# Sliding-window attention and a feed-forward on one core: early loads in float32 on one queue, cast on chip; attention two tiles ahead

## The chip, the core and the metric

The kernel runs on one core of one Trainium2 chip. The metric is device microseconds of one execution. The profile's span (first to last instruction) is about 2 us shorter than that time; 373.34 us of time was a span of 371.6. The engines are named as the profile names them: PE is TensorE, PEld its weight loads, DVE is VectorE, ACT is ScalarE, POOL is GpSimd, SP is the engine that issues most DMAs. PSUM is where both kernels put the results of their matmuls and transposes (pt, ps_s, ps_od, ph and py in the timelines).

## The reference, cut to what matters

```python
# q, k, v: (8 batches, 8 heads, 576 positions, 64), float32
scores = (q @ k.T) / 8                       # per head
scores = where(|i - j| <= 32, scores, -1e9)  # sliding window
attn   = softmax(scores) @ v
x      = attn as (8*576 tokens, 512)
h      = x @ w_in                            # 512 x 2048
out    = gelu_tanh(h) @ w_out                # 2048 x 512, float32 out
```

## The kernel before

Attention works on a batch of 576 tokens, the feed-forward on tiles of 512 tokens. Batch 0's attention runs first, alone. Then tile t of the feed-forward runs with batch t+1's attention scattered between its matmuls. The traces show the work of an engine in the order in which the kernel issues it, so where an instruction is issued decides what it can hold up; x4 below moves the casts of a pair in that order and nothing else, and the pair's loop goes from 7.70 to 6.13 us.

One unit of attention is half of a pair of heads; a batch has four pairs, eight units. The parts that the change and the argument touch:

```python
def cast_pair(b, pr):                 # q and k of a pair, float32 -> float16
    ...
    nc.vector.tensor_copy(q16 or k16, raw q or k)           # two casts, 128x512

def trans_pair(b, pr):                # 8 transposes into one PSUM tile, 2 copies out
    pt = psT.tile([128, 8, 128], FP16, name="pt", tag="T")  # psT: one buffer
    for j in range(4): nc.tensor.transpose(pt[:, j, :], q16[:, j, :, :], idn)
    for j in range(4): nc.tensor.transpose(pt[:, 4 + j, :], k16[:, j, :, :], idn)
    nc.vector.tensor_copy(QTs[b][:, pr, :, 0:128], pt[:, 0:4, :])
    nc.vector.tensor_copy(KTs[b % 2]..., pt[:, 4:8, :]...)

def scores(b, u):                     # psS: one buffer
    ... 6 matmuls into ps_s
    nc.scalar.activation(pe, ps_s, AF.Exp, scale=SCALE)
    nc.vector.tensor_tensor(pm, pe, mask, op=ALU.mult)

def values(b, u):                     # psO: one buffer; row sums come from a matmul with ones
    ... 12 matmuls into ps_od
    nc.scalar.activation(lt, sums, AF.Ln)
    nc.scalar.activation(rt, lt, AF.Exp, scale=-1.0)        # 1 / sum
    nc.vector.tensor_tensor(xT[...], values, rt, op=ALU.mult)

# the start: batch 0
cast_tail(0)
for pr in range(NPAIR):
    cast_pair(0, pr)
    trans_pair(0, pr)
    if pr == 0:
        trans_tail(0)                 # positions 512..575 of all heads, same PSUM buffer
    for u in (2 * pr, 2 * pr + 1):
        scores(0, u)
        if u > 0:
            values(0, u - 1)
values(0, 7)

for t in range(NT):                   # 9 tiles
    b = t + 1
    # input half: 64 matmuls, with the casts and transposes of batch b between them
    # output half: 64 matmuls, with scores and values of batch b between them
    ...
```

q and k come on SP's queue in float32; v, w_in and w_out on GpSimd's queue, whose transfers write float16: a quarter of w_in is 512 KB in the page of before and 1024 KB in that of after, where it comes in float32, and both pages have 36.70 MB read from HBM.

The softmax here doesn't subtract the row's maximum and nothing guards it: scores larger than these inputs give would overflow.

## Time and profile before

| | |
|---|---|
| time | 373.57 us median of 3 runs (373.52 to 374.18) |
| profiled span | 371.6 us, PE busy 338.2 us (91%) |
| first feed-forward matmuls | three at 41.34 us; the rest from 42.88 us, after the last product xT |
| a tile with one batch of attention | 38.40 us, of which 37.88 busy |
| a tile without attention | 27.65 us |

The next lines are the busy time by stretch of the kernel before. The columns are the stretch in us, its length, then busy time and number of instructions of each engine, the granted TensorE clock, the DMA share and GB/s.

```profile
0.00:42.88 42.88, 17.68 (x184) 12.53 (x185) 19.11 (x46) 15.12 (x26) 19.41 (x37) 1.00 1.19 222
42.88:82.18 39.30, 39.23 (x313) 18.81 (x313) 18.17 (x41) 25.32 (x43) 6.90 (x9) 1.00 0.88 115
120.58:158.99 38.41, 37.89 (x310) 18.20 (x308) 18.96 (x42) 25.63 (x42) 4.81 (x7) 1.00 0.56 105
```

The number just after the comma, TensorE's busy time, is what to read: it is idle for 25 of the first 43 us, and for half a microsecond per tile afterwards. So only the start has time to take. What the start waits for is in the timeline of the kernel before. A line has start and duration in us, engine, source line, operation, output and inputs; the bracket is the engine's idle time before it and what ended it.

```profile
24.33 0.46 DVE L238 TENSOR_TENSOR xT<-ps_od,rt 128x288 f16<-128x288 f32 x1 [1.02 <-ACT rt L237]
24.70 0.42 DVE L174 CAST q<-qr 128x512 f16<-128x512 f32 x1
25.04 0.42 DVE L174 CAST k<-kr 128x512 f16<-128x512 f32 x1
25.18 0.61 PE L183 MATMUL pt<-idn,q 128*128 128x128 f16 x4 [1.80 <-DVE q L174]
...
26.25 0.42 DVE L186 COPY QT<-pt 128x512 f16<-128x512 f16 x1 [0.80 <-PE pt L185]
26.60 0.68 DVE L187 COPY KT<-pt 128x512 f16<-128x512 f16 x1
...
27.33 0.53 PE L201 MATMUL ps_s<-QT,KT 64*128 64x160 f16 x6 [1.12 <-DVE KT L187]
...
32.88 0.61 PE L183 MATMUL pt<-idn,q 128*128 128x128 f16 x4 [1.80 <-DVE q L174]
```

The q cast at 24.70 has no bracket: it starts as soon as VectorE is done with the product xT and waits for no data. TensorE in its turn waits 1.80 us for that cast. The pair's loop from transposes to transposes is 32.88 - 25.18 = 7.70 us, all of it latency of small instructions on three engines. The feed-forward follows the loop's end at once, as the chain of the kernel before shows (start, duration, what was worked on):

```profile
40.51 0.92 PE ps_od L228 x12
...
42.88 2.77 PE ph L254 x9
```

The nine matmuls from 42.88 us are not the first. The first twelve need xT, three of them only pairs that were done, and these three run while the last product is still being made. The timeline of the kernel before has all twelve, and then the transposes of batch 1's tail:

```profile
41.34 4.30 PE L254 MATMUL ph<-xT,w_in 128*128 128x512 f16 x12
45.49 0.39 PE L162 MATMUL pt<-idn,t 128*128 128x128 f16 x4
```

The prediction, and the expectations below, count the start of before as 42.88 us. Where this text compares starts, it takes the first matmul of each kernel, 41.34 us here.

### The profile page before, as it was taken

How to read it: one execution, taken by the hardware profiler on the slowest of the kernel's cores; microseconds unless marked ns; L12 is line 12 of the kernel's file. 1: busy time of each engine (PE TensorE's matmuls, PEld its weight loads, DVE VectorE, ACT ScalarE, POOL GpSimd, SP SyncE). 2: the span in 40 equal slices, each digit the busy share in tenths (PEclk: the TensorE clock that was granted, in tenths of full speed). 3: DMA queues.
4: the chain of work that ended last, by engine and by line, in shares of the span. 5: the costliest groups of instructions: out<-in, count | busy, mean ns of one | idle time of the engine just before them, and what ended most of it. 6: DMA issues, size and time to landing. Idle time of an engine off the chain costs nothing.

```text
span 371.6 us, 6392 instructions
## 1 busy us (share of the span) xinstructions
PE 338.2 (91%) x2592; PEld 164.6 (44%) x2592; DVE 156.8 (42%) x347; ACT 214.4 (58%) x352; POOL 45.6 (12%) x67
## 2 busy tenths in 40 slices
PE   0545799999999999999999999999999999999995
PEld 0334354445444444444444544454445444444442
DVE  2554453555354635553545445653545353011011
ACT  1234656676666766677666667656675677612600
POOL 8622121040002200120004000400000000000000
PEclk9999999999999999999999999999999999999999
DMA  9999999159223951197129801991020111013012
GB/s 156 268 246 205 247 211 76 59 67 255 56 56 47 226 105 59 31 201 145 30 58 170 179 28 59 146 202 30 28 58 0 30 30 57 2 30 84 2 37 76
DMA packets 72574, 37.64 MB, mean 101 GB/s; under 512 B 47456, under 2 KB 67936, under 8 KB 72544
## 3 DMA queue, kind: packets, MB, share of 16 engines
q1 hardware_dynamic: 30816, 28.32, 28.0%
q0 software_dynamic: 41728, 8.92, 26.4%
q8 instruction: 20, 0.33, 0.4%
q14 instruction: 10, 0.08, 0.1%
HBM read 36.70 MB, written 9.44 MB: 124 GB/s over the span
## 4 chain that ended last, share of the span: by engine, by line
PE 82%; ACT 9%; DVE 4%; POOL 3%; issue 1%; POOLq 0%
PE py L268 35%; PE ph L254 29%; PE ps_od L228 9%; PE ps_s L201 5%; ACT rt L237 3%; ACT lt L235 2%; ACT L258 2%; PE pt L185 2%; PE pt L183 2%; DVE xT L238 2%; ACT gT L258 1%; POOL V L107 1%; POOL w_in L120 1%; ACT pe L208 1%; POOL mask L129 1%
## 5 line engine op out<-in xcount | busy, mean ns | idle before, releaser
L268 PE MATMUL py<-w_out,gT 128*128 128x512 f16 x576 | 142.9, 381 | 0.0
L254 PE MATMUL ph<-xT,w_in 128*128 128x512 f16 x576 | 135.3, 382 | 3.6 <-ACT gT L258 3.1
L258 ACT ACTIVATE gT<-ph 128x512 f16<-128x512 f32 x144 | 84.5, 597 | 58.5 <-PE ph L254 57.5
L254 PEld LDWEIGHTS <-w_in 128*128 128x128 f16 x576 | 54.6, 98 | 65.2 <-issue 8.2
L208 ACT ACTIVATE pe<-ps_s 128x832 f16<-128x832 f32 x64 | 55.2, 862 | 37.5 <-PE ps_s L201 37.4
L268 PEld LDWEIGHTS <-gT 128*128 128x128 f16 x576 | 47.7, 98 | 51.9
L210 DVE TENSOR_TENSOR pm<-pe,mask 128x832 f16<-128x832 f16 x64 | 37.9, 592 | 61.1 <-ACT pe L208 60.5
L107 POOL DMA_DIRECT2D V<-in_v_dram x32 | 28.5, 894 | 184.2 <-PE ps_od L228 157.9
L235 ACT ACTIVATE lt<-ps_od 128x288 f32<-128x288 f32 x64 | 26.2, 410 | 40.7 <-PE ps_od L228 40.7
L238 DVE TENSOR_TENSOR xT<-ps_od,rt 128x288 f16<-128x288 f32 x64 | 29.3, 458 | 47.7 <-ACT rt L237 47.7
L272 DVE COPY yo<-py 128x512 f32<-128x512 f32 x36 | 24.7, 685 | 49.5 <-PE py L268 49.5
L228 PE MATMUL ps_od<-pm,V 128*64 128x192 f16 (+4 forms) x384 | 35.7, 242 | 4.6 <-DVE xT L238 3.9
L228 PEld LDWEIGHTS <-V 128*64 128x64 f16 x384 | 23.4, 115 | 29.5 <-issue 29.1
L228 PE MATMUL ps_od<-pm,ones 128*64 128x192 f16 (+4 forms) x384 | 32.9, 236 | 0.0
L186 DVE COPY QT<-pt 128x512 f16<-128x512 f16 x32 | 13.6, 425 | 43.1 <-PE pt L185 43.1
L237 ACT ACTIVATE rt<-lt 128x288 f32<-128x288 f32 x64 | 28.3, 443 | 2.0
L201 PE MATMUL ps_s<-QT,KT 64*128 64x192 f16 (+4 forms) x384 | 24.1, 235 | 4.7 <-DVE KT L187 3.3
L183 PE MATMUL pt<-idn,q 128*128 128x128 f16 x128 | 13.3, 230 | 15.2 <-DVE q L174 15.2
L201 PEld LDWEIGHTS <-KT 64*128 64x128 f16 x384 | 12.3, 97 | 29.8 <-issue 25.0
L228 PEld LDWEIGHTS <-ones 128*64 128x64 f16 x384 | 24.0, 117 | 0.0
L187 DVE COPY KT<-pt 128x512 f16<-128x512 f16 x32 | 21.8, 681 | 0.0
L183 PEld LDWEIGHTS <-q 128*128 128x128 f16 x128 | 10.0, 102 | 22.2 <-DVE q L174 15.6
(27 smaller groups left out, 108.1 us busy)
## 6 DMA issues: line engine op xcount, KB each, us to landing
qr<-in_q_dram SPq DMA_DIRECT2D x7, 1024.0 KB, 9.7
kr<-in_k_dram SPq DMA_DIRECT2D x7, 1024.0 KB, 13.6
V<-in_v_dram POOLq DMA_DIRECT2D x32, 128.0 KB, 8.3
w_in<-in_moe_w_in_dram POOLq DMA_DIRECT2D x4, 512.0 KB, 22.8
w_out<-in_moe_w_out_dram POOLq DMA_DIRECT2D x4, 512.0 KB, 30.1
out_dram<-yo SPq DMA_DIRECT2D x8, 256.0 KB, 2.3
out_dram<-yo SPq DMA_DIRECT2D x8, 224.0 KB, 2.4
out_dram<-yo SPq DMA_DIRECT2D x8, 192.0 KB, 2.3
```

What stands on the lines that cost most here:

```text
L107: nc.gpsimd.dma_start(V[:, c, :, :], v[b, :, 128 * c:128 * c + 128, :].rearrange("h p d -> p h d"))
L183: nc.tensor.transpose(pt[:, j, :], q16[:, j, :, :], idn)
L201: nc.tensor.matmul(ps[:, h, off:off + 4 * n].rearrange("k (j p) -> k j p", j=4), KTs[b % 2][r0:r0 + 64, pr, 128 * c:128 * c + 128], QTs[b] ...
L208: nc.scalar.activation(pe, ps[:, :, 0:SW], AF.Exp, scale=SCALE)
L210: nc.vector.tensor_tensor(pm, pe, masks[hf].rearrange("p (o w) -> p o w", o=1).broadcast_to([128, 2, SW]), op=ALU.mult)
L228: nc.tensor.matmul(od[r0:r0 + 64, w, 0:4 * HALF].rearrange("d (j p) -> d j p", j=4)[:, :, a:e], V[:, c, 2 * pr + h, :] if w == 0 else ones ...
L235: nc.scalar.activation(lt, od[:, 1, 0:4 * HALF], AF.Ln)
L237: nc.scalar.activation(rt, lt, AF.Exp, scale=-1.0)
L238: nc.vector.tensor_tensor(xT[:, pr, b * S:(b + 1) * S].rearrange("d (j p) -> d j p", j=4)[:, :, HALF * hf:HALF * hf + HALF], od[:, 0, 0:4 ...
L254: nc.tensor.matmul(ph, w_in16[:, dc, fc * 128:fc * 128 + 128], xT[:, dc, t * 512:(t + 1) * 512], start=(dc == 0), stop=(dc == 3))
L258: nc.scalar.activation(gTs[t][:, fc, :], ph, AF.Gelu_apprx_tanh)
L268: nc.tensor.matmul(py, gTs[t][:, fc, t4 * 128:t4 * 128 + 128], w_out16[:, fc, :], start=(fc == 0), stop=(fc == NF - 1))
```

## The change

Its intent: the early loads (q, k, v of two batches, w_in, w_out) come in float32 on SP's queue in the order in which they are needed, and are cast on chip, mostly on GpSimd. The attention of two batches runs before the feed-forward. The first two tiles share their input half group by group, so that each megabyte of w_in that arrives feeds two tiles. Later, batch t+2 runs within tile t, wholly in its output half. The diff, cut to its core:

```diff
-FIRST, LAG, STEP = 15, 4, 7
+FIRST, STEP, LAG = 8, 6, 10
+TRANS = (0, 13, 25, 37)
+RING = 2048                                  # xT becomes a ring of 2048 tokens
...
-    load_qk(0, 4)
-    load_v(0)                                # and w_in, w_out, batch 1: GpSimd's casting queue
+    load_qk(0, True)                         # by pair on SP: q, k, (tails), v
...
+    load_qk(1, True)
...
+    for b in range(2):
+        cast_tail(b)
+        for pr in range(NPAIR):
+            cast_pair(b, pr, nc.gpsimd)
+            nc.gpsimd.tensor_copy(V..., vr...)          # two casts
+            trans_pair(b, pr)
+            if pr == 0:
+                trans_tail(b)
+            for u in (2 * pr, 2 * pr + 1):
+                scores(b, u)
+                values(the unit before)
+    wi = [load_w_in(0)]
+    cast_w(wi[0], w_in16[:, :, 0:512])       # half VectorE, half GpSimd
+    values(1, 7)
+    for g in range(4):                       # input halves of tiles 0 and 1
+        for t in range(2):
+            for fc in range(4 * g, 4 * g + 4):
+                ffn_in(t, fc)
+                ...                          # next group's load and cast
+    ...                                      # w_out loads and casts, loads of batch 2
     for t in range(NT):
+        if t >= 2:
+            for fc in range(NF): ffn_in(t, fc)
+        b = t + 2
+        cast_tail(b); cast_pair(b, 0)
+        for pr in range(NPAIR):
+            put(TRANS[pr], trans_pair, b, pr)
+            if pr == 0: put(TRANS[pr] + 2, trans_tail, b)
+            if pr < 3:  put(TRANS[pr] + 4, cast_pair, b, pr + 1)
+        for u in range(8):
+            put(FIRST + STEP * u, scores, b, u)
+            put(FIRST + STEP * u + LAG, values, b, u)
+        for i in range(64):                  # output half
+            ...                              # what was put at step i
+            ffn_out(t, i)
```

More of the change, by code (lines that the diff above doesn't have):

```diff
@@ L67 @@
     gp = ctx.enter_context(tc.tile_pool(name="gp", bufs=2))
+    stage = ctx.enter_context(tc.tile_pool(name="stage", bufs=3))
     yp = ctx.enter_context(tc.tile_pool(name="yp", bufs=3))
@@ L84, with load_qk @@
     w_out16 = big.tile([128, NF, DM], FP16, name="w_out16")
-    xT = big.tile([128, NPAIR, NTOK], FP16, name="xT")
+    xT = big.tile([128, NPAIR, RING], FP16, name="xT")
     raws = {}
-    def load_qk(b, split):
+    def load_qk(b, by_pair):
         qr = rawp.tile([128, H, 256], FP32, name="qr")
@@ L93, in load_qk, with main, tail @@
         raws[b] = (qr, kr, tr)
-        step = H // split
-        for h0 in range(0, H, step):
+        def main(h0, h1):
             for src, dst in ((q, qr), (k, kr)):
                 nc.sync.dma_start(
-                    dst[:, h0:h0 + step, :],
-                    src[b, h0:h0 + step, 0:512, :].rearrange("h (p j) d -> p h (j d)", j=4))
-            if h0 == 0:
-                nc.sync.dma_start(tr[0:64, :, :], q[b, :, 512:576, :].rearrange("h s d -> s h d"))
-                nc.sync.dma_start(tr[64:128, :, :], k[b, :, 512:576, :].rearrange("h s d -> s h d"))
+                    dst[:, h0:h1, :],
+                    src[b, h0:h1, 0:512, :].rearrange("h (p j) d -> p h (j d)", j=4))
+        def tail():
+            nc.sync.dma_start(tr[0:64, :, :], q[b, :, 512:576, :].rearrange("h s d -> s h d"))
+            nc.sync.dma_start(tr[64:128, :, :], k[b, :, 512:576, :].rearrange("h s d -> s h d"))
+        if by_pair:
+            vr = stage.tile([128, 5, H, 64], FP32, name="vr", tag="stage")
+            raws[b] = (qr, kr, tr, vr)
+            for h0 in range(0, H, 2):
+                main(h0, h0 + 2)
+                if h0 == 0:
+                    tail()
+                for h in (h0, h0 + 1):
+                    nc.sync.dma_start(vr[:, 0:4, h, :],
+                                      v[b, h, 0:512, :].rearrange("(c p) d -> p c d", p=128))
+                nc.sync.dma_start(vr[0:64, 4, h0:h0 + 2, :],
+                                  v[b, h0:h0 + 2, 512:576, :].rearrange("h p d -> p h d"))
+        else:
+            main(0, H)
+            tail()
     def load_v(b):
@@ L112, with load_w_in, load_w_out, cast_w @@
     w_out_v = moe_w_out.rearrange("(c p) f -> p c f", p=128)
-    load_qk(0, 4)
+    def load_w_in(i):
+        w = stage.tile([128, 4, 512], FP32, name="wst", tag="stage", padded_shape=[128, 5, 512])
+        nc.sync.dma_start(w, w_in_v[:, :, 512 * i:512 * i + 512])
+        return w
+    def load_w_out(i):
+        w = stage.tile([128, 4, 512], FP32, name="wst", tag="stage", padded_shape=[128, 5, 512])
+        nc.sync.dma_start(w, w_out_v[:, 4 * i:4 * i + 4, :])
+        return w
+    def cast_w(w, dst):
+        for c in range(4):
+            (nc.vector if c < 2 else nc.gpsimd).tensor_copy(dst[:, c, :], w[:, c, :])
+    load_qk(0, True)
     nc.gpsimd.memset(idn, 0.0)
@@ L117 @@
                             base=0, pattern=[[-1, 128]], channel_multiplier=1)
-    load_v(0)
-    for i in range(4):
-        nc.gpsimd.dma_start(w_in16[:, :, 512 * i:512 * i + 512], w_in_v[:, :, 512 * i:512 * i + 512])
     for h in range(2):
@@ L138 @@
         assert off == SW
-    for i in range(4):
-        nc.gpsimd.dma_start(w_out16[:, 4 * i:4 * i + 4, :], w_out_v[:, 4 * i:4 * i + 4, :])
     nc.vector.memset(ones, 1.0)
@@ L144 @@
         nc.vector.memset(Vs[i][64:128, 4, :, :], 0.0)
-    load_qk(1, 1)
-    load_v(1)
+    load_qk(1, True)
     halfs = {}
@@ L167, in trans_tail, with cast_pair @@
         nc.vector.tensor_copy(KTs[b % 2][:, :, 512:576], pt[:, :, 64:128])
-    def cast_pair(b, pr):
-        qr, kr, tr = raws[b]
+    def cast_pair(b, pr, eng=None):
+        qr, kr = raws[b][0:2]
         q16 = ap_.tile([128, 4, 2, 64], FP16, name="q16")
@@ L173, in cast_pair @@
         for src, dst in ((qr, q16), (kr, k16)):
-            nc.vector.tensor_copy(
+            (eng or nc.vector).tensor_copy(
                 dst.rearrange("p j h d -> p h j d"),
@@ L189, in trans_pair, with ring_pieces @@
             pt[:, 4:8, :].rearrange("d j p -> d p j"))
+    def ring_pieces(b, hf):
+        rows = []
+        for j in range(4):
+            g, a = b * S + j * NP_ + HALF * hf, 0
+            while a < HALF:
+                pos = (g + a) % RING
+                e = min(HALF, a + RING - pos)
+                rows.append([j, j + 1, a, e, pos])
+                a = e
+        out_rows = []
+        for r in rows:
+            o = out_rows[-1] if out_rows else None
+            if o and o[2:4] == r[2:4] and o[1] == r[0] and r[4] == o[4] + (o[1] - o[0]) * NP_ \
+                    and o[4] + (r[1] - o[0]) * NP_ <= RING:
+                o[1] = r[1]
+            else:
+                out_rows.append(r)
+        return out_rows
     units = {}
@@ L237, in values @@
         nc.scalar.activation(rt, lt, AF.Exp, scale=-1.0)
-        nc.vector.tensor_tensor(
-            xT[:, pr, b * S:(b + 1) * S].rearrange("d (j p) -> d j p", j=4)[:, :, HALF * hf:HALF * hf + HALF],
-            od[:, 0, 0:4 * HALF].rearrange("d (j p) -> d j p", j=4),
-            rt.rearrange("d (j p) -> d j p", j=4), op=ALU.mult)
+        o3 = od[:, 0, 0:4 * HALF].rearrange("d (j p) -> d j p", j=4)
+        r3 = rt.rearrange("d (j p) -> d j p", j=4)
+        for (j0, j1, a, e, pos) in ring_pieces(b, hf):
+            n, w = j1 - j0, e - a
+            if n > 1:
+                dst = xT[:, pr, pos:pos + n * NP_].rearrange("d (j p) -> d j p", p=NP_)[:, :, 0:w]
+            else:
+                dst = xT[:, pr, pos:pos + w].rearrange("d (j p) -> d j p", j=1)
+            nc.vector.tensor_tensor(dst, o3[:, j0:j1, a:e], r3[:, j0:j1, a:e], op=ALU.mult)
     gTs = {}
@@ L254, in ffn_in @@
             nc.tensor.matmul(ph, w_in16[:, dc, fc * 128:fc * 128 + 128],
-                             xT[:, dc, t * 512:(t + 1) * 512],
+                             xT[:, dc, t * 512 % RING:t * 512 % RING + 512],
                              start=(dc == 0), stop=(dc == 3))
@@ L282, in ffn_out @@
                 g = e
-    cast_tail(0)
-    for pr in range(NPAIR):
-        cast_pair(0, pr)
-        trans_pair(0, pr)
-        if pr == 0:
-            trans_tail(0)
-        for u in (2 * pr, 2 * pr + 1):
-            scores(0, u)
-            if u > 0:
-                values(0, u - 1)
-    values(0, 7)
-    begun = False
-    for t in range(NT):
-        b = t + 1
-        att = b < B
-        if att and b + 1 < B:
-            load_qk(b + 1, 1)
-            load_v(b + 1) if b + 1 >= 2 else None
-        if begun:
-            for fc in range(3):
-                ffn_in(t, fc, 3, 4)
-        for fc in range(3 if begun else 0, NF):
-            if att:
-                if fc == 3:
-                    cast_tail(b)
-                    cast_pair(b, 0)
-                    trans_tail(b)
-                if fc in (5, 8, 11, 14):
-                    pr = (fc - 5) // 3
-                    trans_pair(b, pr)
-                    if pr < 3:
-                        cast_pair(b, pr + 1)
-            ffn_in(t, fc)
-        if att:
-            load_exp_table()
-            at = {0: [(scores, 0)]}
-            for u in range(8):
-                if u:
-                    at.setdefault(FIRST + STEP * (u - 1), []).append((scores, u))
-                if u < 7:
-                    at.setdefault(FIRST + LAG + STEP * u, []).append((values, u))
-            for i in range(64):
-                for fn, u in at.pop(i, []):
-                    fn(b, u)
-                ffn_out(t, i)
-            assert not at
-            ffn_in(t + 1, 0, 0, 3)
-            values(b, 7)
-            ffn_in(t + 1, 1, 0, 3)
-            ffn_in(t + 1, 2, 0, 3)
-            begun = True
-        else:
-            for i in range(64):
-                ffn_out(t, i)
-            begun = False
@@ new lines @@
+    for b in range(2):
+        cast_tail(b)
+        V, vr = Vs[b], raws[b][3]
+        for pr in range(NPAIR):
+            cast_pair(b, pr, nc.gpsimd)
+            nc.gpsimd.tensor_copy(V[:, 0:4, 2 * pr:2 * pr + 2, :], vr[:, 0:4, 2 * pr:2 * pr + 2, :])
+            nc.gpsimd.tensor_copy(V[0:64, 4, 2 * pr:2 * pr + 2, :], vr[0:64, 4, 2 * pr:2 * pr + 2, :])
+            trans_pair(b, pr)
[3 more added lines that the diff above has]
+                scores(b, u)
+                if u > 0:
+                    values(b, u - 1)
+                elif b:
+                    values(b - 1, 7)
@@ new lines @@
+    wi = [load_w_in(0)]
+    cast_w(wi[0], w_in16[:, :, 0:512])
+    values(1, 7)
+    for g in range(4):
+        if g < 3:
+            wi.append(load_w_in(g + 1))
+        for t in range(2):
+            for fc in range(4 * g, 4 * g + 4):
+                ffn_in(t, fc)
+                if t == 0 and fc == 4 * g + 1 and g < 3:
+                    cast_w(wi[g + 1], w_in16[:, :, 512 * g + 512:512 * g + 1024])
+    for g in range(4):
+        cast_w(load_w_out(g), w_out16[:, 4 * g:4 * g + 4, :])
@@ new lines, with put @@
+    load_qk(2, False)
+    load_v(2)
+    for t in range(NT):
+        if t >= 2:
+            for fc in range(NF):
+                ffn_in(t, fc)
+        b = t + 2
+        at = {}
+        def put(i, fn, *args):
+            at.setdefault(i, []).append((fn, args))
+        if b < B:
+            load_exp_table()
+            if b + 1 < B:
+                load_qk(b + 1, False)
+                load_v(b + 1)
+            cast_tail(b)
+            cast_pair(b, 0)
+            for pr in range(NPAIR):
+                put(TRANS[pr], trans_pair, b, pr)
+                if pr == 0:
+                    put(TRANS[pr] + 2, trans_tail, b)
+                if pr < 3:
+                    put(TRANS[pr] + 4, cast_pair, b, pr + 1)
+            for u in range(8):
+                put(FIRST + STEP * u, scores, b, u)
+                put(FIRST + STEP * u + LAG, values, b, u)
+        for i in range(64):
+            for fn, args in at.pop(i, []):
+                fn(*args)
+            ffn_out(t, i)
+        assert not at
```

## The prediction

> **What bounds the kernel now.** TensorE, once the feed-forward starts: at 42.88 us in the timeline; the last matmul ends near 367.4, and 4.2 us of copy and store follow. A bare tile (128 matmuls of 128x512) takes 27.65 us; a tile with one batch of attention repeats every 38.40 us, 37.88 of it busy (windows), so a batch costs 10.2 us of TensorE and 0.5 of bubble. Only the first 42.88 us (17.7 busy) has idle time worth taking.
>
> Loads don't bound that start. Attention of batch 0 goes pair by pair, transposes starting at 17.39, 25.18, 32.87 us: 7.7 us a pair. The timeline shows the loop: values, Ln, Exp, xT product, then on the same in-order VectorE the q/k casts, transposes (1.05), QT and KT copies (0.42, 0.68), scores (0.55), Exp (0.86). The q cast follows xT without waiting for data.
>
> **The change at the start.** It moves 15.5 MB of early loads to one queue. I expect little from that: [...] 1 KB packets ran at 300 GB/s alone, 243 beside the cast queue's 30. A pair (832 KB) should land every 4 to 4.5 us, faster than consumed.
> Casts go to GpSimd. [...] this trace has no such cast. First casts near 6.5 us (4.7 us of mask selects come first), first transposes near 8.
> The loop loses only the casts: after values, Ln/Exp/xT until 1.4, QT/KT copies 2.35, scores and Exp 3.85, the other unit's Ln/Exp/xT 5.2, values 6.15. Estimate: 6.15 us a pair, not 7.7. But eight pairs now precede any feed-forward: 8 + 5.8 + 7 x 6.15 + 1 (tails) + 2.4 (end) = **60 us**. Break-even is 42.9 + 10.7 = 53.6, so the start loses 6.5 us. The weights, shared by two tiles, arrive in time; sharing wins nothing.
>
> **Later.** Six batches of attention instead of seven stay inside tiles, all in the output half. Estimated stalls: the tail's transposes come two matmuls after pair 0's but share their one PSUM buffer, so TensorE waits for the QT/KT copies, 0.75 us a batch; VectorE, with 19 us of work in 24, adds 0.15: 0.9 against 0.5. Tile 1 has no input half after tile 0's output half, so batch 3's casts queue behind yo on VectorE: 2 us once.
>
> Sum: 60 + 9 x 27.65 + 6 x (10.2 + 0.9) + 2 + 0.4 + 4.2 = 382 span, plus 2.0 between span and time: **384 us**, 2.7% slower. Range 377 to 391. Chances: faster 0.02, within 2% 0.28, slower 0.70.
>
> **What would show it.** Right: first feed-forward matmul at 57 to 63 us, behind the attention chain, not a weight load; transposes 6 to 6.5 us apart; TensorE nearly full afterwards; tail transposes waiting for KT copies; a 2 us wait for casts at tile 1. Wrong: feed-forward near 50, or transposes waiting for GpSimd casts or landings.
>
> **What would make it wrong.** GpSimd casts over 1.9 us (the pair is then bound by them, 390 or more); 256-byte V packets on one queue slower than 31 ns each; a shorter loop than I chained (5.2 us a pair makes it even); other stalls in the denser output half, 1 us a tile being worth 6.

## The result, and the profile after

The kernel after took 385.42 us (median of 4 runs, 384.81 to 386.21) against 373.7 (4 runs, 373.52 to 374.18). The ratio is 1.0313 (95% interval 1.029 to 1.0336): slower. Ratios here are the mean time of one kernel's runs over that of the other's of the same rounds, so not quite the ratio of the medians.

The chain of the kernel after shows the feed-forward starting behind the attention, at about 59.2 us (its first matmul, in the timeline, is at 59.14):

```profile
58.31 0.90 PE ps_od L278 x12
59.21 28.78 PE ph L309 x128
```

The pair's loop in the timeline of the kernel after, to be held against that of before:

```profile
18.62 0.61 PE L213 MATMUL pt<-idn,q 128*128 128x128 f16 x4
...
19.35 0.61 POOL L204 CAST q<-qr 128x512 f16<-128x512 f32 x1 [1.04 <-PE pt L213]
19.64 0.46 DVE L296 TENSOR_TENSOR xT<-ps_od,rt 128x288 f16<-128x288 f32 x1 [0.88 <-ACT rt L287]
...
20.01 0.41 DVE L216 COPY QT<-pt 128x512 f16<-128x512 f16 x1
20.34 0.68 DVE L217 COPY KT<-pt 128x512 f16<-128x512 f16 x1
21.08 0.53 PE L251 MATMUL ps_s<-QT,KT 64*128 64x160 f16 x6 [1.43 <-DVE KT L217]
...
24.75 0.61 PE L213 MATMUL pt<-idn,q 128*128 128x128 f16 x4
```

The transposes no longer wait for a cast (no bracket at 18.62 and 24.75), and GpSimd is a pair ahead: its q cast at 19.35 waited for the transposes to free a buffer. The loop is 6.13 us. Between 21.08 and 24.75 the same Exp, mask, Ln, Exp and product steps stand as before.

Stretches of the kernel after (columns as before):

```profile
0.00:59.14 59.14, 31.39 (x360) 24.47 (x361) 30.11 (x68) 26.88 (x47) 25.27 (x57) 1.00 0.62 174
59.14:87.83 28.69, 28.69 (x131) 12.79 (x130) 8.99 (x18) 20.64 (x34) 15.87 (x19) 1.00 1.12 320
141.41:179.95 38.54, 37.79 (x309) 18.26 (x308) 18.49 (x45) 25.51 (x43) 4.55 (x7) 1.00 0.54 105
```

TensorE is now idle for 28 us before the feed-forward instead of 25. The two input halves that share the weights run without a gap (28.69 busy of 28.69), and a later tile with attention takes 38.54 us, about what it took before.

The boundary between tile 0's and tile 1's output halves is new. There is no input half between them, so the timeline of the kernel after shows batch 3's casts queued on VectorE behind xT and the output copy yo:

```profile
112.70 0.46 DVE L296 TENSOR_TENSOR xT<-ps_od,rt 128x288 f16<-128x288 f32 x1 [1.56 <-ACT rt L287]
113.07 0.68 DVE L327 COPY yo<-py 128x512 f32<-128x512 f32 x1
113.67 0.42 DVE L184 CAST t<-tr 128x512 f16<-128x512 f32 x1
114.00 0.58 DVE L204 CAST q<-qr 128x512 f16<-128x512 f32 x1
114.50 0.41 DVE L204 CAST k<-kr 128x512 f16<-128x512 f32 x1
114.64 0.40 PE L213 MATMUL pt<-idn,q 128*128 128x128 f16 x4 [1.92 <-DVE q L204]
...
116.48 0.61 PE L192 MATMUL pt<-idn,t 128*128 128x128 f16 x4 [0.68 <-DVE KT L217]
116.88 2.67 PE L323 MATMUL py<-w_out,gT 128*128 128x512 f16 x6
```

The wait of 1.92 us was predicted. What comes after it was not: six matmuls take 2.67 us there, against 1.47 a few microseconds earlier. The stretches of the same kernel say why (the third number from the end is the granted clock):

```profile
117.00:118.00 1.00, 1.00 (x4) 0.34 (x3) 0.87 (x6) 0.00 (x0) 0.00 (x0) 0.50 0.84 236
120.00:121.00 1.00, 1.00 (x8) 0.53 (x7) 0.22 (x1) 0.74 (x1) 0.00 (x0) 1.00 1.05 349
```

The clock record kept with the trace, of which these stretches show the mean, holds one drop to half clock while the kernel computes, from 115.90 us and 3.41 us long, and then full clock again. In the clock records of before and after, the stretches of one clock between the first change and the last are 327.68 us in before and 54.61, 3.41 and 262.83 us in after: 96, 16, 1 and 77 times 3.413 us.

The record also dates the slow first matmuls. It begins at 61.29 us here and at 44.27 us in before, with full clock; up to there the matmuls of the feed-forward follow each other at about 0.43 us, afterwards at 0.22. So full clock is on record from 2.15 us after the first feed-forward matmul here, and from 2.93 us after it in before.

Three lines of the waits of the kernel after (who waited for whom, us in total, times, longest):

```profile
PE pt L192 <- DVE KT L217: 7.0, 8, 1.8
PE pt L213 <- DVE q L204: 1.9, 1, 1.9
POOL V L345 <- DMA vr<-in_v_dram: 3.3, 4, 1.7
```

The first is the tail's transposes waiting for the one PSUM buffer. The second is the boundary. The third is all that the V casts waited for landings in the whole kernel.

### Where the 11.5 us of span went

| term | us | how it is worked out |
|---|---|---|
| later first matmul of the feed-forward | +17.8 | 59.14 - 41.34 |
| one batch fewer inside tiles | -10.8 | before: span after the first matmul 330.3, less 9 x 27.65, the end of 4.2 and 1.6 of slow first matmuls (next but one line), over 7 batches = 10.81 |
| boundary of tiles 0 and 1: wait, then half clock | +4.0 | 1.92, and 26.77 for tile 1's output half with attention against 24.73 in later tiles |
| slow first matmuls of the feed-forward | -0.5 | after: 28.69 - 27.65 = 1.0; before: 4.15 for twelve (41.34 to 45.49), 1.6 more than at full rate (12 x 27.65 / 128) |
| six batches in the denser output half | +1.1 | 6 x (10.99 - 10.81); 10.99 is what is left of the span after |

### The profile page after: what moved, and what is told of

The parts are those of the page before. It is cut to its first block, busy times and chain, and to the rows that moved or that the text cites. A ratio compares the mean times of both kernels' runs of the same rounds, so it can differ in the third digit from the quotient of the medians.

```text
span 383.1 us, 6525 instructions
## 1 busy us (share of the span) xinstructions
PE 343.9 (90%) x2592; PEld 171.8 (45%) x2592; DVE 158.0 (41%) x379; ACT 209.6 (55%) x349; POOL 59.4 (15%) x97
## 4 chain that ended last, share of the span: by engine, by line
PE 81%; DVE 8%; ACT 7%; issue 2%; POOL 1%; DVEq 0%
PE ph L309 33%; PE py L323 31%; PE ps_od L278 8%; PE ps_s L251 5%; DVE xT L296 3%; ACT rt L287 2%; ACT lt L285 2%; DVE KT L217 2%; ACT pe L258 2%; PE pt L213 2%; PE pt L215 2%; DVE QT L216 1%; PE pt L192 1%; POOL mask L164 0%; POOL mask L162 0%
## 5 line engine op out<-in xcount | busy, mean ns | idle before, releaser
L323 PE MATMUL py<-w_out,gT 128*128 128x512 f16 x576 | 147.6, 384 | 0.0
L309 PE MATMUL ph<-xT,w_in 128*128 128x512 f16 x576 | 126.7, 382 | 0.0
L309 PEld LDWEIGHTS <-w_in 128*128 128x128 f16 x576 | 56.5, 98 | 68.7 <-issue 1.4
L323 PEld LDWEIGHTS <-gT 128*128 128x128 f16 x576 | 49.2, 98 | 50.3 <-issue 1.1
L296 DVE TENSOR_TENSOR xT<-ps_od,rt 128x288 f16<-128x288 f32 (+6 forms) x96 | 31.3, 353 | 42.7 <-ACT rt L287 42.6
L278 PE MATMUL ps_od<-pm,V 128*64 128x192 f16 (+4 forms) x384 | 38.2, 253 | 9.1 <-DVE xT L296 8.3
L278 PEld LDWEIGHTS <-V 128*64 128x64 f16 x384 | 25.3, 122 | 32.4 <-issue 26.4
L129 POOL DMA_DIRECT2D V<-in_v_dram x24 | 21.2, 896 | 113.7 <-PE ps_od L278 111.7
L278 PE MATMUL ps_od<-pm,ones 128*64 128x192 f16 (+4 forms) x384 | 35.7, 248 | 0.0
L278 PEld LDWEIGHTS <-ones 128*64 128x64 f16 x384 | 26.0, 124 | 0.0
```

The costliest lines, as they stand in the source:

```text
L278: nc.tensor.matmul(od[r0:r0 + 64, w, 0:4 * HALF].rearrange("d (j p) -> d j p", j=4)[:, :, a:e], V[:, c, 2 * pr + h, :] if w == 0 else ones ...
L296: nc.vector.tensor_tensor(dst, o3[:, j0:j1, a:e], r3[:, j0:j1, a:e], op=ALU.mult)
L309: nc.tensor.matmul(ph, w_in16[:, dc, fc * 128:fc * 128 + 128], xT[:, dc, t * 512 % RING:t * 512 % RING + 512], start=(dc == 0), stop=(dc = ...
L323: nc.tensor.matmul(py, gTs[t][:, fc, t4 * 128:t4 * 128 + 128], w_out16[:, fc, :], start=(fc == 0), stop=(fc == NF - 1))
```

## The experiments

Nine kernels ran, all correct. Each was timed in three rounds against the kernel before on the same chip (x1 to x4 on one chip, x5 to x8 on a second, x9 on a third; the medians of before differ by 0.3 us at most). No interval contains 1. With a threshold of 2%, the record calls x1 and x3 slower, x2 and x5 unclear, and the other five the same; all gains below are about 2% or less.

| run | us, median (range) | before, median | ratio (95%) |
|---|---|---|---|
| x1_early_casts | 382.9 (382.84 to 383.37) | 373.32 | 1.0259 (1.0236 to 1.0282) |
| x2_tail_later | 380.55 (378.78 to 381.36) | 373.32 | 1.0201 (1.0168 to 1.0234) |
| x3_vector_casts | 397.1 (396.18 to 397.7) | 373.32 | 1.0635 (1.0607 to 1.0662) |
| x4_before_cast_ahead | 369.25 (368.26 to 369.61) | 373.32 | 0.9887 (0.9861 to 0.9912) |
| x5_before_trans_ahead | 366.62 (365.84 to 366.92) | 373.26 | 0.9816 (0.9795 to 0.9837) |
| x6_one_ahead | 367.67 (366.84 to 368.46) | 373.26 | 0.984 (0.9816 to 0.9864) |
| x7_after_trans_ahead | 368.23 (367.22 to 369.28) | 373.26 | 0.9863 (0.9834 to 0.9892) |
| x8_one_ahead_trans_ahead | 367.8 (367.6 to 367.98) | 373.26 | 0.9851 (0.9833 to 0.9868) |
| x9_one_ahead_split_casts | 367.5 (366.73 to 368.95) | 373.07 | 0.9853 (0.9822 to 0.9885) |

The theory: the start is a chain of latencies of one pair after another; the change shortened the pair by taking the casts out of VectorE's order, but doubled the number of pairs ahead of the feed-forward. The main rival: loads bound the start of before, and the order of the loads is what changed the pair.

### x3_vector_casts: undo the casts on GpSimd alone

```diff
-            cast_pair(b, pr, nc.gpsimd)
+            cast_pair(b, pr)                 # VectorE, in its old place
```

> The kernel after, with only the q and k casts of the start put back on VectorE in their old place; loads, V casts, two tiles ahead stay. Theory: the pair's loop was shortened only because the casts left VectorE's in-order queue: the distance of the transposes goes back from 6.13 to about 7.6 us, the feed-forward starts near 70 us instead of 59, 396 us. Rival: the loads in order of need on one queue shortened the pair: the distance stays near 6.1 and the time near 385.

Measured: 397.1 us. The timeline of this run has the old wait of the transposes back, 7.69 us apart; the feed-forward starts at 71.40 us.

```profile
23.22 0.61 PE L213 MATMUL pt<-idn,q 128*128 128x128 f16 x4 [1.80 <-DVE q L204]
30.91 0.61 PE L213 MATMUL pt<-idn,q 128*128 128x128 f16 x4 [1.80 <-DVE q L204]
```

The new loads stayed and the pair went back to its old length. So it was the casts' place in VectorE's order that shortened the pair, not the order of the loads. The loads did move the first pair: its transposes started at 7.63 us, with casts on VectorE as in before, where they started at 9.78 because the tail's cast had waited for its landing until 8.74.

### x4_before_cast_ahead: the same gain without the loads or GpSimd

```diff
+    cast_pair(0, 0)
     for pr in range(NPAIR):
-        cast_pair(0, pr)
         trans_pair(0, pr)
         if pr == 0:
             trans_tail(0)
+        if pr < 3:
+            cast_pair(0, pr + 1)             # VectorE, but one pair ahead
```

> The kernel before, loads and engines untouched; the start's q/k casts of the next pair are only issued on VectorE right after the transposes' copies of this pair, one pair ahead. Theory: the loop loses the casts' place, so the pair takes 6.15 instead of 7.7 us, three pairs, the feed-forward starts at 38.3 instead of 42.9: 369.0 us. Rival: loads bound the start of the kernel before: no gain, 373.6, and the transposes or the feed-forward wait for landings.

Measured: 369.25 us. The timeline of this run has the transposes 6.13 us apart, without a wait:

```profile
15.99 0.61 PE L183 MATMUL pt<-idn,q 128*128 128x128 f16 x4
...
22.12 0.61 PE L183 MATMUL pt<-idn,q 128*128 128x128 f16 x4
```

This is the loop of the kernel after, to a hundredth, on the loads and the engines of the kernel before. The rival falls for the pair: after the first pair, nothing in the start of before waited for loads at this pace. The first pair did (its transposes started at 10.06 us, with the loads of before). The feed-forward's first matmul came at 36.76 us, 4.6 earlier than in before, as expected for three pairs. The first twelve matmuls took 5.0 us (to 41.77) instead of 4.15; so 0.9 us of the 4.6 were lost again. The median is 4.1 us lower.

### x1_early_casts: take the boundary's wait away

```diff
-            cast_tail(b)
-            cast_pair(b, 0)
+            if t != 1:
+                cast_tail(b)
+                cast_pair(b, 0)
+            if t == 0:
+                put(52, cast_tail, 3)        # inside tile 0's output half
+                put(52, cast_pair, 3, 0)
```

> The kernel after, with batch 3's first casts (tail, first pair) issued inside tile 0's output half at step 52 instead of behind tile 0's last yo copy. In the kernel after TensorE waited 1.92 us there and then ran 3.4 us at half clock. Theory: the wait is what let the clock drop, so both go: about 2 + 1.9 = 4 us less, 381.5 us, and the granted clock stays 1.0 from the feed-forward's start to its end. Rival: the drop of the clock has another cause (load, time since start): then only the wait goes, 383.5 us, and the half clock is still there near 117 us.

Measured: 382.9 us, 2.5 less than after: between the two. The stretch just behind the boundary, first in after, then in this run:

```profile
117.00:120.40 3.40, 3.40 (x16) 1.13 (x15) 1.48 (x7) 0.52 (x1) 0.00 (x0) 0.66 0.97 304
```

```profile
117.00:120.40 3.40, 3.40 (x32) 1.65 (x30) 2.10 (x5) 1.54 (x2) 0.00 (x0) 1.00 1.08 253
```

Both the wait of 1.92 us and the half clock are gone, as the theory said. But the moved casts delayed the product xT on VectorE: TensorE waits 0.46 us for it at 112.02, and the tail's transposes wait 1.15 us instead of 0.68. The casts took a slot that was not free, which gave about 0.9 us back. Another 0.4 us had been lost before the boundary. The size expected was too large by that.

### x2_tail_later: take away the tail's wait

```diff
-                    put(TRANS[pr] + 2, trans_tail, b)
+                    put(TRANS[pr] + 7, trans_tail, b)
```

> The kernel after, with the tail's transposes seven matmuls after the first pair's instead of two. Theory: TensorE waits for the one PSUM transpose buffer, 0.7 us in each of six tiles, and that wait just goes: a tile with attention 37.85 us instead of 38.54, 381.2 us in all. Rival: another wait takes its place (VectorE is nearly full in the output half, so the later tail copies delay scores or products): under 1 us gained, 384.5 or more.

Measured: 380.55 us, 4.9 less than after. In the chain of this run the input halves of later tiles are 37.68 us apart instead of 38.54:

```profile
138.48 13.81 PE ph L309 x64
...
176.16 13.81 PE ph L309 x64
```

The wait went and nothing took its place. This run also says something of the clock. The boundary's wait of 1.93 us is still there, yet the profiled run had no half clock behind it: its page has PEclk 9 in every slice, and its granted clock from 117 to 118 us is 1.00, where that of after is 0.50. In after TensorE was busy for 1.38 us of the 3.41 us just ahead of the drop (112.49 to 115.90). In x3 the clock fell too: its wait of 1.93 us ended at 126.78, and the page has PEclk 8 in the slice from 128.4 us. Why it fell in these two and not in x2 is not shown; no run moved the wait to test it. The four times were 378.78, 381.36, 381.26 and 379.83 us, at mean granted clocks of 0.999, 0.993, 0.993 and 0.998. They do not settle what a drop costs: only the first was profiled, and in after the run at 0.998 (385.09 us) was no faster than the one at 0.994 (384.81).

### x5_before_trans_ahead: shorten the loop further, loads of before

```diff
-    for pr in range(NPAIR):
-        cast_pair(0, pr)
-        trans_pair(0, pr)
-        if pr == 0:
-            trans_tail(0)
-        for u in (2 * pr, 2 * pr + 1):
-            scores(0, u)
-            if u > 0:
-                values(0, u - 1)
+    cast_pair(0, 0)
+    trans_pair(0, 0)
+    trans_tail(0)
+    cast_pair(0, 1)
+    for u in range(8):
+        scores(0, u)
+        if u > 0:
+            values(0, u - 1)
+        if u % 2 == 0 and u < 6:
+            trans_pair(0, u // 2 + 1)
+            if u < 4:
+                cast_pair(0, u // 2 + 2)
```

> The kernel before, loads and engines untouched; in the start the casts, transposes and copies of the next pair are issued between this pair's units, so only scores, Exp, values, Ln, Exp and product remain in the loop. Theory (the start is a chain of latencies): a unit every 2.45 us instead of 3.85, values of unit 0 at about 15 us as in the run with casts ahead, feed-forward at about 33.5 us, 365.5 us. Rival (loads bind below 38 us): the feed-forward starts no earlier than 36 or its first tile waits for weights or batch 1, 368.5 us or more.

Measured: 366.62 us, the fastest median. The feed-forward starts at 33.06 us:

```profile
33.06 4.99 PE L254 MATMUL ph<-xT,w_in 128*128 128x512 f16 x12
...
37.88 0.39 PE L162 MATMUL pt<-idn,t 128*128 128x128 f16 x4
```

That is 8.3 us earlier than in before, and the median is 6.6 lower. The twelve first matmuls take 4.8 us (33.06 to 37.88) instead of 4.15. The chain of waits of this run now leads through loads: it passes 24.73 us of a V load of batch 1 that lands at 56.9 us. At this start, loads begin to bind, though TensorE waited only 0.38 us for that landing.

### x6_one_ahead: undo the two tiles ahead, keep the new loads and casts

The tiles of the kernel before (attention of batch t+1 in tile t) behind the start of the kernel after, cut to batch 0. The queue's order is batch 0, half of w_in, batch 1's q and k, the rest of w_in, w_out. All weight casts are on GpSimd.

```diff
-    for b in range(2):
+    wi = [load_w_in(0), load_w_in(1)]
+    ...                                      # b = 0 only, same pair loop
+    load_v(1)                                # GpSimd's casting queue
+    load_qk(1, False)
+    for g in range(4):
+        if g >= 2:
+            wi.append(load_w_in(g))
+        cast_w(wi[g], w_in16[:, :, 512 * g:512 * g + 512])
+    for g in range(4):
+        cast_w(load_w_out(g), w_out16[:, 4 * g:4 * g + 4, :])
+    values(0, 7)
+    ...                                      # the tiles of before
```

> The kernel after with the two tiles ahead undone: float32 loads of batch 0 and the weights in order of need on one queue and casts on GpSimd as in after (the weights' casts all on GpSimd), the pair loop of after, but one batch ahead and the tiles of before. Theory: what made the change slower is eight pairs ahead of the feed-forward instead of four; the start's own part is a gain. Feed-forward at about 33.4 us (in after, batch 0 ends there), the tiles as before: 364.5 us. Rival: one queue and casts on chip cost as much as they give: 370 us or more.

Measured: 367.67 us. The sign and most of the size are the theory's: with four pairs ahead the same loads, casts and loop give a gain of 1.6% instead of a loss of 3.1%. The expected 364.5 was missed by 3.2 us. The expectation counted from 42.88 us; from the first matmul of before, 41.34, a start at 33.4 gains 1.5 us less. The feed-forward started at 34.81 us, not 33.4: the fourth pair's transposes came 7.9 us after the third's instead of 6.1. The timeline of this run shows the place, a mask product on VectorE that took 2.73 us where 0.59 is usual, while GpSimd was casting w_in without a break:

```profile
21.72 5.27 POOL L147 CAST w_in<-wst 128x512 f16<-128x512 f32 x8
22.31 2.73 DVE L258 TENSOR_TENSOR pm<-pe,mask 128x832 f16<-128x832 f16 x1 [1.52 <-ACT pe L256]
```

The same is seen in x8 (2.46 us at 23.81) and, smaller, in after (1.44 us at 41.83). When both engines cast weights at once in after (64.12 to 65.77 us), a pair of casts took 1.18 us on VectorE and 1.62 on GpSimd, against 0.75 on VectorE at 58.17 and 1.17 on GpSimd at 45.60, where only one of them cast. No run moved the casts of w_in alone, so that they caused the longer mask products is not shown. And the twelve first matmuls took from 34.81 to 40.03 us, 1.1 more than in before.

### x7_after_trans_ahead: two tiles ahead with the shorter loop

The edits of x1 and x2, and in the start the loop of x5 over sixteen units (casts still on GpSimd):

```diff
+    for n in range(16):
+        b, u = n // 8, n % 8
+        scores(b, u)
+        if n:
+            values((n - 1) // 8, (n - 1) % 8)
+        if u % 2 == 0 and n < 14:
+            ...                              # casts and trans_pair of the next pair
```

> The kernel after, two tiles ahead kept, with the pair loop shortened (casts, transposes and copies of the next pair between this pair's units) plus the two repairs of the runs with early casts and later tail. Theory: 16 units at 2.45 us, feed-forward near 50 us instead of 59: 9 less, the repairs give 2.5 and 5: 369 us. Two tiles ahead then neither gains nor loses much against before. Rival: loads (two batches must land first) hold the shorter loop up: feed-forward at 54 or later, 373 us or more.

Measured: 368.23 us, feed-forward at 50.03 us: both as expected. The kernel after was slow by its loop and its two waits, not by its loads: two batches landed in time for a start nine microseconds earlier.

### x8_one_ahead_trans_ahead: one ahead with the shorter loop

The start of x6 with the loop of x5; nothing else differs from x6.

> The one-ahead kernel with early float32 loads, with the shortened pair loop. Theory: values of unit 0 at 11.7 us as in after, units at 2.45 us, feed-forward at 30 us; [...]w_out may hold the output half of tile 0 up by some 3 us: 363 us, range 360 to 366. Rival: loads and casts on GpSimd bind earlier, and it is no faster than the one-ahead kernel without the shortened loop.

Measured: 367.8 us, a miss. The feed-forward did start at 29.90 us, five microseconds before x6, and the time did not move. The timeline of this run shows where it went:

```profile
52.14 0.38 PE L321 MATMUL py<-w_out,gT 128*128 128x512 f16 x1 [0.54 <-POOL w_out L147]
53.45 0.38 PE L321 MATMUL py<-w_out,gT 128*128 128x512 f16 x1 [0.94 <-POOL w_out L147]
...
55.55 1.89 PE L321 MATMUL py<-w_out,gT 128*128 128x512 f16 x4
```

The output half of tile 0 waits for w_out, 2.0 us in five waits, and then runs slower: four matmuls in 1.89 us where 1.04 is usual, and the page has PEclk 8 in the slice from 54.9 us. The rival, that the loads and casts bind, is what happened; the theory's allowance of 3 us was too small.

### x9_one_ahead_split_casts: more hands for the casts

The kernel of x8, with half of the casts of the last two w_out groups on VectorE, batch 1's V loads after the first two w_in groups' casts, and batch 2's loads behind the weights. The second w_out group is also cast later, inside tile 0's input half.

```diff
-    load_v(1)
...
+        if g == 1:
+            load_v(1)
...
+            if t == 0 and fc == 15:
+                for g in (2, 3):
+                    for c in range(4):
+                        (nc.vector if c < 2 else nc.gpsimd).tensor_copy(
+                            w_out16[:, 4 * g + c, :], wo[g][:, c, :])
+                load_qk(2, False)
+                load_v(2)
```

> The one-ahead kernel with the shortened pair loop, in which tile 0's output half waited for GpSimd's casts of w_out (0.2 to 0.9 us four times, and the half clock that followed). Here half of the casts of the last two w_out groups go to VectorE, batch 1's V loads come after the first two w_in groups' casts instead of before, and batch 2's loads after the weights. Theory: the feed-forward still starts at 30 us and those waits go, 2 to 4 us less: 364.5 us. Rival: all 15.5 MB land no earlier, so the wait only moves to the landing of w_out or of batch 1's V: 367 us or more.

Measured: 367.5 us, no better. The rival was right. The waits of this run from 26 to 60 us:

```profile
DVE w_out L398 <- DMA wst<-in_moe_w_out_dram: 5.5, 2, 3.4
...
PE py L321 <- DVE w_out L398: 2.9, 4, 1.7
```

The feed-forward started at 28.64 us, TensorE waited for the casts, and the casts for the landing of w_out. Four different starts, from 28.6 to 34.8 us, ended between 366.6 and 367.8 us (x5, x6, x8, x9). Below a start of about 33 us, what the pair loop gives is taken back in tile 0. From its first matmul to that of tile 1, tile 0 took 38.47 us in before, 39.72 in x5, 39.54 in x6, 43.60 in x8 and 45.19 in x9.

## Why the prediction was right, point by point

- **The bound.** Right for the loop. The start of before was latency and not loads: x4 shortened it by 4.6 us without touching a load, and x3 lengthened that of after with all the new loads in place. Only the first pair waited for a landing; the new loads brought its transposes from 9.78 to 7.63 us (x3). And 42.88 us, which the prediction takes for the start of the feed-forward, is its fourth matmul.
- **The pair.** Predicted 6.15 us, measured 6.13, and 7.7 again with the casts back (x3). The casts on GpSimd took 0.61 us (median of 16 in after). The prediction had no run to take their time from, so its 8 us for the first transposes is the author's estimate. Their time did not matter in the loop: GpSimd waited for buffers (1.04 us at 19.35, 2.10 at 25.48).
- **Start of the feed-forward.** Predicted 60 us, measured 59.14. The first transposes came at 6.40 us instead of 8, since the first cast began at 5.73 instead of 6.5 and they waited for that one alone. What followed took 0.5 us more than the terms of the prediction add up to; batch 1's first two pairs took 7.02 and 6.62 us, the first with the tail, the second with a mask product of 1.44 us.
- **Break-even.** Predicted a loss of 6.5 us at the start, counted from 42.88; on that count it is 16.3 - 10.8 = 5.5, and from first matmul to first matmul 17.8 - 10.8 = 7.0. That more batches ahead is the loss, and the rest of the start a gain, is shown by x6.
- **Sharing of the weights.** It had nothing to gain: in before the feed-forward's start did not wait for a weight (the chain leads through the attention). In after the shared input halves ran without a gap.
- **Output half.** The tail's wait was predicted at 0.75 us and was 0.68 to 0.69; x2 removed it, and 0.86 us a tile with it. The bubbles of a tile with attention were predicted at 0.9 us and are 38.54 - 37.79 = 0.75. So the denser half cost 1.1 us in all and not 2.4.
- **The boundary.** The wait of 2 us was predicted (1.92 measured). That TensorE then runs at half clock for 3.41 us was not; the term came to 4.0 us. x1 removed both together.
- **Sum.** 382 predicted, 383.1 measured as span; 384 and 385.42 us as time. The first-matmul loss at the feed-forward's start was put at 0.4 us and was 1.0. That the sum fits to 1 us is in part luck: the start (-0.9) and the six batches (-0.7) came cheaper than predicted, the boundary (+2.0) and the first matmuls (+0.6) dearer.
- **The load path.** The expectation that one queue brings little bandwidth was not tested by itself; the packet records of before have 1 KB packets at about 300 GB/s alone (2.8 to 3.6 us), and at 243 beside 30 on the casting queue (14 to 16 us). What the runs show is that the order and engine of the loads were not what moved the pair (x3, x4). They moved the first pair: its transposes started at 9.65 to 10.06 us with the loads of before (before, x4, x5), and at 6.40 to 7.63 with the new ones.

What stays open: whether GpSimd's casts are what stretched the mask products of x6 and x8, and what decides whether a wait of 1.9 us is followed by half clock.

## What to carry to other kernels

Before moving work to another engine, look for a free slot on the one it is on: one pair of casts issued earlier on VectorE gave the same loop as a whole new load path with GpSimd. Here a pair of attention cost its full latency ahead of TensorE's first feed-forward matmul, 6.1 us, and 10.81 / 4 = 2.7 us inside a tile, little more than its busy time there (10.2 / 4), so run as little ahead as the first tile needs. When a start becomes shorter, ask what lands last: here the gains stopped at a start near 33 us, where the weights and the next batch took over.
